# Three edits to a fused linear attention and bilinear feed-forward kernel: last block in pieces, paired early products, one block's stores on another queue

## The chip, the cores and the metric

The kernel runs on one core of a Trainium2 chip. The metric is device time in microseconds of one execution. The kernel before takes 296.92 us, the median of 6 runs (296.78 to 297.49).

## What is computed

Eight batches, eight heads, 576 positions, head size 64. Attention without a softmax, a normalisation per head, then a feed-forward part in which two projections are multiplied:

```python
kv  = einsum('bhsd,bhse->bhde', k, v)
o   = einsum('bhsd,bhde->bhse', q, kv)
o   = o / sqrt(mean(o*o, -1) + 1e-6) * g_norm
x   = o.transpose(0, 2, 1, 3).reshape(4608, 512)
out = ((x @ w_a) * (x @ w_b)) @ w_out        # 512 -> 1536 -> 512
```

Inputs and output are float32; the kernel multiplies in bfloat16 and float16 and sums in float32.

## The kernel before, in words

**Blocks.** The 4608 tokens are worked through in nine blocks of 512. Block 0 goes the plain way (`std_block`, line 387, and `o_std`, line 943). Blocks 1 to 8 use a fast 2x2 scheme with seven products instead of eight, called p1 to p7: `wino_block` (line 839) for x @ w_a and x @ w_b, and `o_unit` (line 1008) for the last product. The seven products need sums and differences of their operands, which VectorE makes beforehand: lines 746 (weights), 806 (tokens) and 993 (products of the two projections; four for each chunk, in the order s3, a21, s2, s4). ScalarE copies product banks out (`ev`, line 1040, and line 420), VectorE adds a bank to what was copied (`comb`, lines 1046 and 858).

**The output unit.** In `o_unit`, p6 is added in TensorE's bank on top of p1 after the bank has been copied out, p7 on top of p6, p3 on top of p5. The four output quarters are c11 = p1 + p2, c12 = p1 + p6 + p3, c21 = p1 + p6 + p7 + p4, c22 = p1 + p6 + p7 + p5. Each of the seven products has 12 matmuls of 128x256: two row halves ("subs") of six. The last block passes extra banks `W`, and takes the branch `if W:` (lines 1065 to 1093). There p7's sum is copied out by ScalarE (`e3`), p5's by ScalarE into `u5` (line 1076), and the quarters end with c22, c21 in two row halves, and c12 whole. `put` stores the quarters.

**Attention.** Batches 0 and 1 are loaded in a layout of 96 partitions (`early_batch`); TensorE transposes q (`early_qT_mm`, line 341, 12 transposes for a pair of heads) and multiplies k by v (`early_kv_mm`, line 325, 12 matmuls for a pair). Batches 2 to 7 are loaded by `load_node` over GpSimd's queue: q goes through a DRAM scratch tensor `scr` (line 661), k (lines 667, 668) and v (lines 673, 677) come straight. SyncE then turns the scratch into `qT` by a transposing DMA (line 682). The next batch's loads wait on GpSimd until `qT` of the batch before has landed (line 656). TensorE multiplies k by v (line 624), then q by the result (lines 353 and 539); ScalarE and VectorE normalise (lines 363, 371, 376).

**Order of the work.** The order on every engine is set by a small planner, `Plan`. Each piece is a node with an engine, a duration in us, a priority, what it depends on and the buffers that it takes and frees. `Plan.order` always picks the node that can start first on its engine, and among nodes that can start at once the one with the lowest priority number; the program is then written in that order, and each engine runs its part strictly in that order. `LAT` is the time that the planner adds between a node's end and its users. `EARLY_AT`, `W_AT`, `q_us` and `kv_us` are arrival times of data that the planner assumes. The semaphores of the real program are not touched by these numbers: they change the order alone.

**Banks.** The eight PSUM banks belong to three pools: banks 0 to 3 (rings `RX` and `RY`, two tiles each at most), bank 4 (`RO`), and banks 5 to 7 (`RQ` and `RS`, two each at most).

**Stores of block 0.** `o_std` stores four tiles of 128 rows on SyncE (line 964, through `store`, line 911). Because batch 0 has the 96-partition layout, each tile falls into two stores, eight in all.

Of the kernel before, what the change touches and what calls it, by code (L numbers as in the profile page):

```python
# [70 lines left out]


class Plan:
    LAT = {"PE": 0.27, "SP": 2.2, "ACT": 0.2, "DVE": 0.18}
    OWN = {"ACT": 0.12, "DVE": 0.13}

    def __init__(self, t0):
# [60 lines left out]
def kernel(  # L138
# [11 lines left out]
    nc = tc.nc  # L150
# [31 lines left out]
    NJ = FC // 2  # L182
# [226 lines left out]
    def act_us(n, bias=False):  # L409
        return (0.155 if bias else 0.06) + n / 1200  # L410
# [10 lines left out]
        ]  # L421

    T0 = 20.0
    B5, B6, CX, CY = 5, 8, 3, 4
    TB, TURN, AHEAD = 5, 3.0, 8.0
    plan = Plan({"PE": 5.7, "DVE": 3.3, "ACT": 2.7, "SP": 5.0, "POOL": 22.5, "V": 0.0})
# [62 lines left out]
    def early_batch(b, win):  # L489
        at = Attn(b)  # L490
        at.qt = [Buf(RKD).take()]
        at.kvd = at.qt[0].tile
        w0, w1 = win
        done = {}
        for p in range(NP):
            pr = w0 + (w1 - w0) * (p - 0.7) / NP
            sq, sk = (Buf(RX), Buf(RY)) if b == 0 else (Buf(RQ), Buf(RS))
            got = {n: plan.at(t) for n, t in zip("qkv", EARLY_AT[b][p])}
            if b == 0 and p == 0:
                for n in "qkv":  # L500
                    cast, eng, us = (
                        (nc.scalar.copy, "ACT", 0.75) if n == "k" else (nc.vector.tensor_copy, "DVE", 0.55)
                    )
                    got[n] = plan.add(
                        eng, us, pr - 1,
                        lambda n=n, cast=cast: cast(early[0][n][:, 0:2], raw[n]),
                        [got[n]],
                    )
            n1 = plan.add(
                "PE", 0.45, pr, lambda p=p, s=sq: at.early_qT_mm(p, s.tile), [got["q"]], [sq]  # L510
            )
            cp, eng, us = (nc.scalar.copy, "ACT", 0.56) if p % 2 and b else (nc.vector.tensor_copy, "DVE", 0.38)
            n2 = plan.add(
                eng, us, pr, lambda p=p, s=sq, cp=cp: at.early_qT_out(p, s.tile, cp),
                [n1], (), [sq],
            )
            n3 = plan.add(
                "PE", 0.40, pr, lambda p=p, s=sk: at.early_kv_mm(p, s.tile),
                [got["k"], got["v"]], [sk],
            )  # L520
            n4 = plan.add(
                "ACT", 0.45, pr,
                lambda p=p, s=sk: at.early_kv_out(p, s.tile, nc.scalar.copy), [n3], (), [sk],
            )
            done[p] = [n2, n4]
        slices(at, win, lambda p: done[p])
# [123 lines left out]
    def load_node(b, prio, dep, xt=None):  # L650
        ld = {"k": Buf(RK), "v": Buf(RV), "q": Buf(RQT)}
        scr = scr_pool.tile([NP, S, 2, D], BF16, name="scr", tag="scr")

        def issue():
            if dep is not None:
                nc.gpsimd.tensor_copy(gate_t, dep["q"].tile[0:1, 0, 0:1])
            if xt is not None:
                nc.gpsimd.tensor_copy(gate_t, xcols(NP - 1, (b - 2) * S, 1)[0:1])
            qv = q[b].rearrange("(p hl) s d -> hl s p d", hl=2)
            for hl in range(2):  # L660
                nc.gpsimd.dma_start(  # L661
                    out=scr[:, :, hl, :].rearrange("p s d -> s p d"), in_=qv[hl]
                )
            kt = ld["k"].tile
            ks = k[b, :, 0:SA, :].rearrange("h (sp c) d -> sp h c d", c=NCH)
            for c in range(NCH):
                nc.gpsimd.dma_start(out=kt[:, c], in_=ks[:, :, c, :])  # L667
            nc.gpsimd.dma_start(out=kt[0:SB, NCH], in_=k[b, :, SA:S, :].rearrange("h sp d -> sp h d"))
            for n, src in (("v", v),):
                t = ld[n].tile[:, 0 : H * (NCH + 1) * D].rearrange(  # L670
                    "p (h c d) -> p h c d", h=H, d=D
                )
                nc.gpsimd.dma_start(
                    out=t[:, :, 0:NCH, :],
                    in_=src[b, :, 0:SA, :].rearrange("h (sp c) d -> sp h c d", c=NCH),
                )
                nc.gpsimd.dma_start(
                    out=t[0:SB, :, NCH, :], in_=src[b, :, SA:S, :].rearrange("h sp d -> sp h d")
                )

        def transpose():
            nc.sync.dma_start_transpose(
                out=ld["q"].tile[:].rearrange("p a s -> p (a s)"),
                in_=scr[:].rearrange("a s h d -> (a s) (h d)"),
            )

        issue_us, q_us, ld["kv_us"] = (15.4, 4.3, 13.0) if dep is None else (9.0, 5.0 if b == 3 else 1.8, 16.0 if b == 3 else 13.0)

        ld["n"] = plan.add(
            "POOL", issue_us, prio, issue, ([(dep["qn"], 8.0)] if dep else []) + ([(xt, TURN)] if xt else []), [ld["k"], ld["v"]]  # L690
        )
        ld["qn"] = plan.add(
            "SP", 2.5, prio, transpose, [(ld["n"], q_us)], [ld["q"]]
        )
        return ld
# [234 lines left out]
    def o_std(ab, muls, win):  # L930
        w0, w1 = win
        ob = Buf(ROS)
        ng, copied = N0 // 128, []
        for g in range(ng):
            pr = w0 + (w1 - w0) * g / ng
            ps = Buf((RO, RY)[g % 2])

            n1 = None
            for f0 in range(0, FC, OP):

                def mm(g=g, ps=ps, f0=f0):
                    for fc in range(f0, f0 + OP):
                        nc.tensor.matmul(  # L943
                            ps.tile[:],
                            lhsT=ab.tile[:, fc, g * 128 : (g + 1) * 128],
                            rhs=wo_t[:, fc, :],
                            start=(fc == 0),
                            stop=(fc == FC - 1),
                        )

                n1 = plan.add(
                    "PE", mm_us(OP, d_model), pr + 0.01 * f0, mm,
                    [(wo_n, 5.8 if f0 + OP <= FC // 2 else 10.6), n1] + [muls[fc] for fc in range(f0, f0 + OP)],
                    [ps] if f0 == 0 else [], [ab],
                )
            o_reads.append(n1)
            n2 = plan.add(
                "ACT", act_us(d_model), pr,
                lambda g=g, ps=ps: nc.scalar.copy(ob.tile[:, g], ps.tile[:]),
                [n1] + copied[-1:], [ob] if g == 0 else [], [ps],  # L960
            )
            copied.append(n2)
            plan.add(
                "SP", 0.45, pr + 1, lambda g=g: store(g * 128, ob.tile[:, g]), [n2], (), [ob]
            )

    def o_unit(r0, ab, muls, osum, pr, du, chunks, pieces, m, w, first, second, X, Y, Z, ob, s2, s3, s4, W):
# [95 lines left out]
        t2, t3, t4 = (so_t[:, i] for i in range(3))  # L1063
        n1, n2, n3, n4 = osum
        if W:
            u5 = Buf(RU)
            p1 = prod(0, X, a11, b11, True, [], [X])
            e1 = ev(0, 0, 0, p1, [ob])
            p2 = prod(1, Y, a12, b21, True, [], [Y])
            c11 = comb(1, 0, 0, Y, [p2, e1], [Y])  # L1070
            p6 = prod(2, X, sx(s2), t2, False, [e1, n2], (), [s2], 2)
            e2 = ev(2, 0, 1, p6)
            p5 = prod(3, Z, a21, t1, True, [n1], [Z], (), 1)
            e5 = plan.add(
                "ACT", act_us(m * EH), pr + 3 * du,
                lambda: nc.scalar.copy(u5.tile[:, every], bank(Z, every)), [p5], [u5],
            )
            p7 = prod(4, X, sx(s3), t3, False, [e2, n3], (), [s3], 0)
            e3 = ev(4, 1, 0, p7)
            c22 = comb(4, 1, 1, X, [p7, e5], [X, u5], u=u5)  # L1080
            p3 = prod(5, Z, sx(s4), b22, False, [e5, n4], (), [s4], 3)
            c12 = comb(5, 0, 1, Z, [p3, e2], [Z])
            e1s, e2s = slice(0, EH), slice(EH, d_model)
            put(0, every, [c11], es=e1s)
            put(1, every, [c22], es=e2s)
            for i in range(m):
                put(0, slice(i, i + 1), [c12], queue=("SP", "ACT")[i], es=e2s)
            for i in range(m):
                subs = slice(i, i + 1)
                p4 = prod(6 + 0.1 * i, W[i], a22, t4, True, [n4], [W[i]], subs=subs)  # L1090
                c21 = comb(6 + 0.1 * i, 1, 0, W[i], [p4, e3], [W[i]], subs)
                put(1, subs, [c21], queue=("ACT", "SP")[i], es=e1s)
            return
        p1 = prod(0, X, a11, b11, True, [(wo_n, 10.6)], [X])
        e1 = ev(0, 0, 0, p1, [ob])
# [45 lines left out]
    for bi in range(1, nb + 1):  # L1141
# [10 lines left out]
        ab, muls = wino_block(bi, (st[bi], st[bi + 1]), wsum)  # L1152
    o_block(
        nb, ab, muls, osum, (st[nb + 1], st[nb + 1] + o_us[nb]), NJ // 2,
        (RO, RY, RY, RS, RQ), NJ // 2,
    )
    order, t = plan.order(), 5.7
    for n in order:
# [34 lines left out]
```

## Time and profile before

| | us |
|---|---|
| median of 6 runs | 296.92 |
| the profiled execution | 296.81 |
| its span, first to last instruction | 294.7 |
| outside the span | 2.1 |
| TensorE busy | 287.5 (98%) |
| VectorE busy | 240.1 (81%) |
| ScalarE busy | 191.5 (65%) |
| GpSimd busy | 77.3 (26%) |
| granted TensorE clock | 1.000 |

How to read it: PE is TensorE, PEld its weight loads, DVE VectorE, ACT ScalarE, POOL GpSimd, SP SyncE. In a timeline, a line starts with the start and the length in us of a run of like instructions; "SPq" is the issuing queue of SyncE. The duration of one matmul there includes its way through the array: those of 256 columns follow each other every 0.109 us although one is 0.273 us long. In the chain of waits, the chain that ended last, a line stands for the stretch that it adds to the path, so there the gap to the next line is counted and not the overlap.

### The profile page before, as it was taken

The page shows a single profiled execution, that of the slowest core. Times are in us where ns is not written, and L with a number is a line of the kernel's source. Part 1 is how long each engine was busy: PE and PEld are TensorE (multiplying, and loading weights), DVE is VectorE, ACT ScalarE, POOL GpSimd, SP SyncE. Part 2 cuts the span into 40 slices and gives each one's busy share as a digit, 9 for nine tenths or more (in the row PEclk, how much of TensorE's full clock was granted, in tenths as well). Part 3 has the DMA queues.
Part 4 walks back from the last instruction along what each step waited for, and adds up shares of the span by engine and source line. Part 5 has one row for each costly group of instructions (what it writes and reads, how often), then busy time and mean ns, then how long its engine had stood idle before and what let it go on. Part 6 is the DMA issues. An engine that isn't in the chain of part 4 may idle for free.

```text
span 294.7 us, 6757 instructions
## 1 busy us (share of the span) xinstructions
PE 287.5 (98%) x2646; PEld 237.8 (81%) x2648; DVE 240.1 (81%) x441; ACT 191.5 (65%) x395; POOL 77.3 (26%) x96
## 2 busy tenths in 40 slices
PE   7999999999999999999999999999999999999993
PEld 3645558965888988899988999898988888888882
DVE  5454879893987988789979999979989958788852
ACT  3757667866578677877757866786769546665420
POOL 8945830940191470380001910000000000000000
PEclk9999999999999999999999999999999999999999
DMA  8999999899999899599716999330165001200053
GB/s 178 199 199 200 196 158 167 114 169 186 207 102 168 139 179 170 43 140 209 170 32 148 143 167 168 81 145 20 40 84 166 2 0 44 101 2 0 9 172 107
DMA packets 112643, 36.26 MB, mean 123 GB/s; under 512 B 89060, under 2 KB 108516, under 8 KB 112612
## 3 DMA queue, kind: packets, MB, share of 16 engines
q0 software_dynamic: 77552, 18.44, 66.4%
q1 hardware_dynamic: 34448, 16.70, 26.6%
q10 hardware_dynamic: 612, 0.71, 0.8%
q8 instruction: 20, 0.33, 0.5%
q14 instruction: 11, 0.09, 0.1%
HBM read 37.75 MB, written 14.75 MB: 178 GB/s over the span
## 4 chain that ended last, share of the span: by engine, by line
PE 88%; DVE 4%; DMA 3%; POOL 2%; issue 1%; ACT 1%; DVEq 0%; ACTq 0%; POOLq 0%
PE bk L839 48%; PE bk L1008 24%; PE bk L387 7%; PE bk L943 3%; DMA wb_t<-in_moe_w_b_dram 3%; PE bk L624 2%; PE bk L353 1%; PE bk L367 1%; POOL as L242 1%; PE bk L539 1%; DVE c L858 1%; POOL so L242 1%; PE bk L341 1%; DVE so L746 1%; DVE o_sb L1046 1%
## 5 line engine op out<-in xcount | busy, mean ns | idle before, releaser
L858 DVE TENSOR_TENSOR c<-bk,u 128x512 f16<-128x512 f32 x144 | 96.4, 687 | 19.3 <-PE bk L839 11.8
L420 ACT COPY u<-bk 128x512 f32<-128x512 f32 x144 | 81.4, 591 | 36.5 <-PE bk L839 30.0
L839 PE MATMUL bk<-xp,wa_t 128*128 128x256 f16 x288 | 55.0, 273 | 0.1
L839 PE MATMUL bk<-xp,wb_t 128*128 128x256 f16 x288 | 55.0, 273 | 0.0
L839 PEld LDWEIGHTS <-wa_t 128*128 128x128 f16 x384 | 37.1, 98 | 5.7 <-issue 0.3
L1008 PEld LDWEIGHTS <-abt 128*128 128x128 f16 x384 | 37.5, 98 | 4.7 <-issue 0.3
L839 PEld LDWEIGHTS <-wb_t 128*128 128x128 f16 x384 | 37.6, 98 | 4.3
L1008 PE MATMUL bk<-wo_t,abt 128*128 128x256 f16 x288 | 37.2, 273 | 0.1
L839 PE MATMUL bk<-T,sb 128*128 128x256 f16 x192 | 36.6, 273 | 0.0
L839 PE MATMUL bk<-T,sa 128*128 128x256 f16 x192 | 36.6, 272 | 0.0
L420 ACT CAST c<-bk 128x512 f16<-128x512 f32 x48 | 28.0, 587 | 12.1 <-PE bk L839 11.5
L893 DVE TENSOR_TENSOR abt<-c 128x1024 f16<-128x1024 f16 x48 | 32.8, 687 | 0.9
L839 PEld LDWEIGHTS <-sb 128*128 128x128 f16 x288 | 28.2, 98 | 3.3
L839 PEld LDWEIGHTS <-sa 128*128 128x128 f16 x288 | 27.9, 98 | 3.5
L1008 PEld LDWEIGHTS <-as 128*128 128x128 f16 x288 | 28.1, 98 | 3.3
L1040 ACT COPY o_sb<-bk 128x512 f32<-128x512 f32 x31 | 18.2, 586 | 18.5 <-PE bk L1008 18.0
L376 DVE SCALAR_TENSOR_TENSOR xp<-bk,g_col,rs 128x288 f16<-128x288 f32 x40 | 20.3, 514 | 10.9 <-ACT rs L371 10.9
L1008 PE MATMUL bk<-so,as 128*128 128x256 f16 x192 | 25.2, 273 | 0.0
L371 ACT ACTIVATE rs<-bk,eps_t 128x288 f32<-128x288 f32 x40 | 20.0, 505 | 6.3 <-PE bk L367 6.1
L667 POOL DMA_DIRECT2D k_t<-in_k_dram x24 | 21.2, 900 | 0.8 <-issue 0.5
L661 POOL DMA_DIRECT2D scr<-in_q_dram x12 | 19.6, 1636 | 2.0 <-DMA wb_t<-in_moe_w_b_dram 0.9
L1046 DVE TENSOR_TENSOR o_sb<-bk,o_sb 128x512 f32<-128x512 f32 (+1 forms) x25 | 16.5, 666 | 3.0 <-PE bk L1008 2.3
(107 smaller groups left out, 428.5 us busy)
## 6 DMA issues: line engine op xcount, KB each, us to landing
out_dram<-o_sb SPq DMA_DIRECT2D x20, 256.0 KB, 2.7
scr<-in_q_dram POOLq DMA_DIRECT2D x12, 288.0 KB, 7.7
k_t<-in_k_dram POOLq DMA_DIRECT2D x24, 128.0 KB, 8.0
v_t<-in_v_dram POOLq DMA_DIRECT2D x6, 512.0 KB, 10.8
out_dram<-o_sb SPq DMA_DIRECT2D x18, 128.0 KB, 2.4
wa_t<-in_moe_w_a_dram POOLq DMA_DIRECT2D x6, 256.0 KB, 10.6
wb_t<-in_moe_w_b_dram POOLq DMA_DIRECT2D x6, 256.0 KB, 10.8
wo_t<-in_moe_w_out_dram POOLq DMA_DIRECT2D x2, 768.0 KB, 9.7
```

The source lines that it names most:

```text
L371: nc.scalar.activation(rs, self.s_ps[p, h][:, 0:HF], AF.Abs_reciprocal_sqrt, bias=eps_t)
L376: nc.vector.scalar_tensor_tensor(out=xcols(p, self.b * S + h * HF, HF), in0=self.x_ps[p, h][:, 0:HF], scalar=g_col, in1=self.rs[p, h], op0 ...
L387: nc.tensor.matmul(ps[:, 0:n], lhsT=w[:, kc, fc * 128 : (fc + 1) * 128], rhs=xcols(kc, 0, n), start=(kc == 0), stop=(kc == KC - 1),)
L420: ("ACT", act_us(n), lambda: nc.scalar.copy(*args())),
L661: nc.gpsimd.dma_start(out=scr[:, :, hl, :].rearrange("p s d -> s p d"), in_=qv[hl])
L667: nc.gpsimd.dma_start(out=kt[:, c], in_=ks[:, :, c, :])
L839: nc.tensor.matmul(ps.tile[:, i * n : (i + 1) * n], lhsT=lhs(w, sm)[:, kc, :], rhs=rhs()[:, kc, :], start=start and i == 0 and kc == 0, st ...
L858: lambda: nc.vector.tensor_add(cs(fi, h), full(ps), u.tile),
L893: nc.vector.tensor_mul(t, c[:, :, :, 0], c[:, :, :, 1])
L1008: nc.tensor.matmul(ps.tile[:, sub * EH : (sub + 1) * EH], lhsT=lhs(slice(j, j + 1))[:, 0, sub * 128 : (sub + 1) * 128], rhs=rhs[:, j, :], ...
L1040: lambda: nc.scalar.copy(o(fi, h), bank(X, every)), [dep], takes, frees,
L1046: nc.vector.tensor_add(o(fi, h, subs), bank(ps, subs), other)
```

## The change

**Tail in pieces.** In the last block's branch, p7 gets a bank `V` of its own and moves from place 4 to place 2.5 in the priorities; ScalarE's copy `e3` goes, and VectorE makes `c2x` = p7 + (p1 + p6) into the c21 quarter instead. p5 and p3 are done in two row halves in two banks `Z[0]`, `Z[1]`, p5's copy in two halves too. c22 becomes an addition of two SBUF operands, `c2x` and `u5`. p4 stands before p3, and c12 is made and stored in two halves, one on ScalarE's queue, one on SyncE's. The block takes seven banks instead of five.

**Two pairs at a time.** For batch 1, the transposes of two pairs of heads become one node (24 transposes), and the k-v products of two pairs too.

**Block 0's stores.** They go from SyncE to GpSimd's queue, with a planned 1.2 us each and a planned latency of 6.0. The planner's `kv_us` for batch 3 goes from 16.0 to 14.0.

```diff
-    LAT = {"PE": 0.27, "SP": 2.2, "ACT": 0.2, "DVE": 0.18}
+    LAT = {"PE": 0.27, "SP": 2.2, "ACT": 0.2, "DVE": 0.18, "POOL": 6.0}
...
+    P7_AT = 2.5
...
-            n1 = plan.add(
-                "PE", 0.45, pr, lambda p=p, s=sq: at.early_qT_mm(p, s.tile), [got["q"]], [sq]
-            )
+            if b == 0:
+                n1 = plan.add(
+                    "PE", 0.45, pr, lambda p=p, s=sq: at.early_qT_mm(p, s.tile), [got["q"]], [sq]
+                )
+            elif p % 2 == 0:
+                sq2 = Buf(RQ)
+                n1 = plan.add(
+                    "PE", 0.9, pr,
+                    lambda p=p, s=sq, s2=sq2: (at.early_qT_mm(p, s.tile), at.early_qT_mm(p + 1, s2.tile)),
+                    [got["q"]], [sq, sq2],
+                )
+            else:
+                sq = sq2
...
+            elif p % 2 == 0:
+                sk2 = Buf(RS)
+                n3 = plan.add(
+                    "PE", 0.8, pr,
+                    lambda p=p, s=sk, s2=sk2: (at.early_kv_mm(p, s.tile), at.early_kv_mm(p + 1, s2.tile)),
+                    [got["k"], got["v"]], [sk, sk2],
+                )
+            else:
+                sk = sk2
...
-        issue_us, q_us, ld["kv_us"] = (15.4, 4.3, 13.0) if dep is None else (9.0, 5.0 if b == 3 else 1.8, 16.0 if b == 3 else 13.0)
+        issue_us, q_us, ld["kv_us"] = (15.4, 4.3, 13.0) if dep is None else (9.0, 5.0 if b == 3 else 1.8, 14.0 if b == 3 else 13.0)
...
-                "SP", 0.45, pr + 1, lambda g=g: store(g * 128, ob.tile[:, g]), [n2], (), [ob]
+                "POOL", 1.2, pr + 1, lambda g=g: store(g * 128, ob.tile[:, g], nc.gpsimd), [n2], (), [ob]
...
-            u5 = Buf(RU)
+            u5, V, Z = Buf(RU), W[0], [Z, W[1]]
+            W = W[2:]
+            rows = [slice(i, i + 1) for i in range(m)]
...
-            e2 = ev(2, 0, 1, p6)
-            p5 = prod(3, Z, a21, t1, True, [n1], [Z], (), 1)
-            e5 = plan.add(
-                "ACT", act_us(m * EH), pr + 3 * du,
-                lambda: nc.scalar.copy(u5.tile[:, every], bank(Z, every)), [p5], [u5],
-            )
-            p7 = prod(4, X, sx(s3), t3, False, [e2, n3], (), [s3], 0)
-            e3 = ev(4, 1, 0, p7)
-            c22 = comb(4, 1, 1, X, [p7, e5], [X, u5], u=u5)
-            p3 = prod(5, Z, sx(s4), b22, False, [e5, n4], (), [s4], 3)
-            c12 = comb(5, 0, 1, Z, [p3, e2], [Z])
+            e2 = ev(2, 0, 1, p6, (), [X])
+            p7 = prod(P7_AT, V, sx(s3), t3, True, [n3], [V], [s3], 0)
+            c2x = plan.add(
+                "DVE", dve_us(m * EH), pr + 4 * du,
+                lambda: nc.vector.tensor_add(o(1, 0), bank(V, every), o(0, 1)), [p7, e2], (), [V],
+            )
+            e5 = []
+            for i in range(m):
+                p5 = prod(3 + 0.1 * i, Z[i], a21, t1, True, [n1], [Z[i]], (), 1, subs=rows[i])
+                e5.append(
+                    plan.add(
+                        "ACT", act_us(EH), pr + 3 * du,
+                        lambda i=i: nc.scalar.copy(u5.tile[:, rows[i]], bank(Z[i], rows[i])),
+                        [p5], [] if i else [u5],
+                    )
+                )
+            c22 = plan.add(
+                "DVE", dve_us(m * EH), pr + 4.2 * du,
+                lambda: nc.vector.tensor_add(o(1, 1), o(1, 0), u5.tile[:, every]), [c2x] + e5, (), [u5],
+            )
...
             for i in range(m):
-                put(0, slice(i, i + 1), [c12], queue=("SP", "ACT")[i], es=e2s)
+                p4 = prod(5 + 0.1 * i, W[i], a22, t4, True, [n4], [W[i]], subs=rows[i])
+                c21 = comb(5 + 0.1 * i, 1, 0, W[i], [p4, c22], [W[i]], rows[i])
+                put(1, rows[i], [c21], queue=("ACT", "SP")[i], es=e1s)
             for i in range(m):
-                subs = slice(i, i + 1)
-                p4 = prod(6 + 0.1 * i, W[i], a22, t4, True, [n4], [W[i]], subs=subs)
-                c21 = comb(6 + 0.1 * i, 1, 0, W[i], [p4, e3], [W[i]], subs)
-                put(1, subs, [c21], queue=("ACT", "SP")[i], es=e1s)
+                p3 = prod(6 + 0.1 * i, Z[i], sx(s4), b22, False, [e5[i], n4], (), [s4], 3, subs=rows[i])
+                c12 = comb(6 + 0.1 * i, 0, 1, Z[i], [p3, e2], [Z[i]], rows[i])
+                put(0, rows[i], [c12], queue=("ACT", "SP")[i], es=e2s)
...
-        (RO, RY, RY, RS, RQ), NJ // 2,
+        (RO, RY, RS, RY, RS, RQ, RY), NJ // 2,
```

More of the change, by code (lines that the diff above doesn't have):

```diff
@@ L516, in early_batch @@
             )
-            n3 = plan.add(
-                "PE", 0.40, pr, lambda p=p, s=sk: at.early_kv_mm(p, s.tile),
-                [got["k"], got["v"]], [sk],
-            )
+            if b == 0:
+                n3 = plan.add(
+                    "PE", 0.40, pr, lambda p=p, s=sk: at.early_kv_mm(p, s.tile),
+                    [got["k"], got["v"]], [sk],
+                )
+            elif p % 2 == 0:
+                sk2 = Buf(RS)
+                n3 = plan.add(
+                    "PE", 0.8, pr,
[4 more added lines that the diff above has]
+                sk = sk2
             n4 = plan.add(
```

## The prediction

> **What bounds the kernel now.** I read the page's busy times first, then the chain of waits by time, then the timeline at the three places that the diff touches.
>
> ```profile
> PE 287.5 (98%) x2646; PEld 237.8 (81%) x2648; DVE 240.1 (81%) x441; ACT 191.5 (65%) x395; POOL 77.3 (26%) x96
> PE 88%; DVE 4%; DMA 3%; POOL 2%; issue 1%; ACT 1%; DVEq 0%; ACTq 0%; POOLq 0%
> ```
>
> TensorE (PE) is busy nearly always, and 88% of the chain lies on it. From 16.2 us, when the first weights are there, to 289.66, when its last matmul ends, it hardly pauses. The exceptions that I find are the places where it goes from small products back to block 0's, one gap at 80.66 to 80.93 behind a VectorE (DVE) chain, and a like one at 225.7. So a change can win in three ways only: less time on TensorE, fewer such gaps, or a shorter end after 289.66. The span ends at 294.7, thus 5.0 us come behind the last matmul.
>
> The chain of waits at the end:
>
> ```profile
> 280.28 8.09 PE bk L1008 x74
> ...
> 288.39 0.59 ACT o_sb L1040
> ...
> 289.01 1.02 DVE o_sb L1046 x2
> 290.03 0.33 DVEq L1188
> 290.36 0.60 DVE o_sb L1046
> ```
>
> The reader is to see that TensorE is packed (74 matmuls in 8.09 us, 0.109 each) up to 288.37, and that the end then does not hang on its last 12 matmuls (p3, to 289.66) but on ScalarE's copy of p7 and VectorE's queue behind it. The timeline, with narrow windows for the last additions:
>
> ```profile
> 288.19 1.47 PE L1008 MATMUL bk<-wo_t,as 128*128 128x256 f16 x12
> 289.01 0.69 DVE L1046 TENSOR_TENSOR o_sb<-bk,u 128x512 f32<-128x512 f32 x1 [3.80 <-ACT o_sb L1040]
> 289.62 0.41 DVE L1046 TENSOR_TENSOR o_sb<-bk,o_sb 128x256 f32<-128x256 f32 x1
> 290.28 0.68 DVE L1046 TENSOR_TENSOR o_sb<-bk,o_sb 128x512 f32<-128x512 f32 x1
> 290.11 1.29 ACTq L911 DMA_DIRECT2D out_dram<-o_sb  x2
> ```
>
> c22 at 289.01, c21 in halves at 289.62 and 289.95, c12 at 290.28 to 290.96: c12's product was there at 289.66, and it waits 0.62 us for VectorE and then takes 0.68. Slots, start to start, are 0.60 for 512 columns and 0.33 for 256.
>
> **Part 1, the tail.** TensorE's count stays: seven products of 12 matmuls. Removed is ScalarE's copy of p7 (0.58); p5's copy (0.58) becomes two, each priced between 0.36 (the nearest short ScalarE copy, L639) and 0.58. Added on VectorE is c2x (0.69, one slot of 0.60); c12 becomes two halves of 0.41. The SBUF-only c22 has no row; between 0.42 (a 512-column float16 sum) and 0.69 (a float32 one with a PSUM operand) I take 0.69, the row of its own type.
>
> p7 in a bank of its own needs no copy of p6 before it, and s3 is the first sum that VectorE makes (282.29 to 282.71), so p7 can be done well before the end. With p4 and p3 last, 24 matmuls or 2.62 us follow p5. VectorE's queue behind p5 is: second half copy 0.36, c22 0.60, two halves of c21 0.66, first half of c12 0.33, in all 1.95. It is 0.67 us ahead of TensorE, so the last half of c12 starts when p3 ends: 289.66 + 0.02, plus 0.41, gives 290.09 instead of 290.96, a gain of 0.87.
>
> Six or fewer matmuls of p4 done earlier, as filling work, cost nothing; each further one brings p5 0.109 closer to the end, and all twelve leave a gain of 0.87 - 0.65 = 0.22. Before, p4 did fill (8 of its 12 before 282.5), because p2 had to wait for a bank of 0 to 3. Now p5's halves have banks 5 to 7, so 8 matmuls of p5 are there to fill instead; I take no loss.
>
> Behind the additions: stores of 128 KB landed after 1.7 to 2.2 us. Six of them were issued between 289.73 and 291.5; now four are out before the last half. That is worth 0 to 0.3; I take 0.05. ScalarE's queue holds only the two stores behind c21 and c12, SyncE's last one waits for nothing else. **Sum: -0.9, between -0.2 and -1.2.**
>
> **Part 2, pairs.** The chain of waits around batch 1's transposes:
>
> ```profile
> 20.55 0.49 PE bk L341 x12
> 21.04 0.97 PE bk L387 x4
> 22.00 0.49 PE bk L341 x12
> 22.49 1.40 PE bk L387 x6
> ...
> 40.95 2.16 PE bk L387 x10
> ```
>
> Ten matmuls of L387 take 2.16, so one takes 0.216. Behind each run of transposes the next run is longer than that: 0.97 - 0.86 and 1.40 - 1.30, 0.10 each time; at 31.45 and 32.69 the same. The transposes themselves cost 0.49 either way. Two runs in one spare one return, twice: -0.2. The k-v products were already 24 in a row (23.89 and 33.66), so there the change finds nothing. The second pair's transposes need a second bank of 5 to 7 at 30.9: if it is the one that VectorE frees at 31.77 and not the one that ScalarE frees at 31.22, TensorE, which gets there at 31.45, waits 0.3. Nothing else hides it: TensorE has its weights over a microsecond ahead (issued 23.17, landing after 10.8, used at 35.30). **Sum: -0.2, between -0.2 and +0.1.**
>
> **Part 3, the stores.** SyncE's and GpSimd's (POOL's) timelines:
>
> ```profile
> 67.45 0.79 SPq L911 DMA_DIRECT2D out_dram<-o_sb  x2
> 68.36 6.03 SPq L682 DMA_TRANSPOSE qT<-scr  x1
> 74.48 4.32 SPq L911 DMA_DIRECT2D out_dram<-o_sb  x6
> ```
>
> ```profile
> 66.47 0.69 POOL L677 DMA_DIRECT2D v_t<-in_v_dram  x1 [1.31 <-DMA scr<-in_q_dram]
> 79.94 0.38 POOL L656 COPY gate_t<-qT 1x1 bf16<-1x1 bf16 x1 [12.79 <-DMA qT<-scr]
> ```
>
> GpSimd has nothing to do from 67.16 to 79.94. Eight issues there cost 0.69 to 0.82 each (rows of L677 and L704), 5.5 to 6.6 in all. They wait for ScalarE's four copies, of which the last ends at 75.51; two issues behind it end at 77.1. Queued behind them is only the gate of batch 4's loads, which waits for batch 3's qT until 79.94 anyway: cover 2.8 us. The tile that they read is wanted again only for block 2. On SyncE the transposing DMA can start when the scratch has landed (issued 55.37, 12.4 to landing: 67.8), 0.6 earlier at most; nobody on the path waits for it.
>
> The page "DMA: Bandwidth & Descriptors" of the Trainium skill, section "SWDGE vs HWDGE vs iDMA", speaks against this edit: a plain transfer belongs on SyncE's or ScalarE's queue, since GpSimd writes its descriptors in software and VectorE can lock it out meanwhile; "SBUF — State Buffer" tells of 620 ns that became 3100. By that the eight issues would be an estimated 25 us, end past 92 and push batch 4's loads by over 12 us. The trace does not agree: from 55 to 60 us GpSimd's issues ran beside a VectorE that was 90% busy, at 0.88 each as elsewhere.
>
> The planned 14.0 moves batch 3's k-v products up by 2.0, from 79.11 to about 77.1. The last piece of V was issued at 66.47 and landed after 10.7, at 77.2; other V loads took 8.9 to 11.7, so 75.4 to 78.2. The stores no longer share the DMA engines ahead of it. TensorE waits 0 to 1.1; I take 0. Against that, the gap of 0.27 at 80.66 may close, as batch 3's products are then there to fill it. **Sum: 0, between -0.3 and +1.1.**
>
> **Total.** -0.9 - 0.2 + 0 = -1.1. Against the profiled execution, 296.81 (294.7 of span and 2.1 around it), that is 295.7; the median lies 0.11 higher, at 296.92, and gives 295.8.
>
> **Rivals.** About 0.2%, or 0.6 us, is what can be told from no change: 296.33 to 297.51.
>
> *V is late.* TensorE stands before batch 3's k-v products until 78.2 instead of 77.1: -1.1 + 1.1, the time stays at 296.9. For it speaks the margin of -0.1; against it the lighter DMA load. Chance 0.07.
>
> *The tail's queue stays on VectorE.* All of p4 fills early, p5 and c22 come late, the tail gains 0.22: 296.92 - 0.2 - 0.2 = 296.5. For it: p4 did fill before. Against it: four products stand ahead of it now. Chance 0.07. This is also the case in which the change does not do what it says.
>
> *Slower: batch 3's normalising crowds VectorE.* From 72.4 to 82.0 VectorE works without a pause and the chain of waits runs through it (72.36 to 80.89) until TensorE gets its input at 80.93. If batch 3's attention comes earlier, its eight normalising operations (L376, slot 0.43, now from 85.12 on) can come in front of the sums that TensorE waits for. Each costs 0.43 there; from four on, +1.7 eats the gain and leaves 296.92 - 1.1 + 1.7 = 297.5; all eight would give 299.2. Against it: qT lands at 79.3 at the earliest, and two microseconds earlier brings them to 83. Chance 0.14, with any other disorder that a newly planned order brings in at this point.
>
> *More:* the gap at 80.66 closes (-0.27) and the last stores land 0.25 sooner: 295.3. Chance 0.10.
>
> **Numbers.** The forecast has 0.62. Faster by over 0.2%: 0.62 + 0.10 = 0.72. Within: 0.07 + 0.07 = 0.14. Slower: 0.14. The range is 295.0 to 297.6: below, the best case with 0.3 to spare; above, the start of the slower case, most of whose 0.14 I leave out.
>
> **What would show it.** After: no ScalarE copy behind p7; the last VectorE addition has 256 columns and starts within 0.1 us of the last matmul's end; last matmul to span's end 4.1 instead of 5.0. Around 21 and 31 us, 24 transposes in one run of 0.98. Eight issues of L911 on GpSimd between 67 and 77.5, the gate at 79 to 80. Wrong would be a TensorE pause at 77, a last matmul later than 289.7, or a changed tail order with p4 ahead of p5.

## The result, and the profile after

The changed kernel takes 298.47 us (median of 17 runs, 297.59 to 300.71), the kernel before 297.17 in the same sessions (36 runs). The ratio is 1.0049, 95% interval 1.0037 to 1.0061: slower by 0.5%, where 1.1 us faster was forecast. The profiled execution took 297.98, its span is 296.2 against 294.7.

The page of the changed kernel, busy times and the chain's shares:

```profile
PE 287.2 (97%) x2646; PEld 237.7 (80%) x2648; DVE 241.2 (81%) x443; ACT 192.9 (65%) x395; POOL 82.3 (28%) x104
PE 68%; DMA 22%; POOL 4%; ACT 1%; DVE 1%; issue 1%; DVEq 0%; ACTq 0%; SPq 0%; POOLq 0%
```

TensorE has the same 2646 matmuls and the same busy time; what is new is that 22% of the chain that ended last is now DMA, where it was 3%. The last part of it in the chain of waits (start, length, what):

```profile
54.02 1.58 POOL scr L682
55.60 12.20 DMA scr<-in_q_dram
...
67.86 14.04 DMA qT<-scr
...
81.95 0.41 PE bk L353 x2
```

Batch 3's transposing DMA is issued at 67.86, lands 14.0 later, and TensorE's first q product of batch 3 starts when it has landed. Before, the same DMA took 11.5 and TensorE did not wait for it. (Lines have moved: 353 is as before, 600 is now 621, 656 is 677, 839 is 860, 911 is 932, 1008 is 1029, 1040 is 1061, 1046 is 1067; in this chain 682 is the load of q, formerly 661, and the transposing DMA is 703.) TensorE's timeline at that place:

```profile
80.14 0.38 PE L860 MATMUL bk<-T,wb_t 128*128 128x256 f16 x2
81.95 0.41 PE L353 MATMUL bk<-qT,kvd 128*128 128x288 bf16 x2 [1.43 <-DMA qT<-scr]
```

Two matmuls from 80.14 have their slots (0.109 each) until 80.36. TensorE then stands for 1.6 us, although "PE busy" for 80 to 85 us, 3.57 of 5, shows less of it, because the last matmul counts as busy for its whole 0.273 us and not for its slot alone. Such pauses are best taken from starts: the next start, less the last start, less one slot. All of them above 0.06 us, behind the first weights, give this account of the two profiled executions:

| us | before | after | difference |
|---|---|---|---|
| first transposes of batch 1 start | 20.48 | 20.75 | +0.27 |
| pauses at batch 1's transposes and products | 12 of 0.09 to 0.10 | 8 | -0.38 |
| pause at 80 | 0.27 | 1.60 | +1.33 |
| pauses at 193 | 0.07 | 0.93 | +0.86 |
| pause at 227 | 0.27 | 0.22 | -0.05 |
| last matmul starts | 289.39 | 291.37 | +1.98 |
| from there to the span's end | 5.27 | 4.83 | -0.44 |
| outside the span | 2.15 | 1.78 | -0.37 |

The first row is scatter of the first loads (20.5 to 21.1 in the runs below). The rest sums to +1.76 for TensorE, -0.44 for the tail and -0.37 outside the span. The last is no scatter: outside the span every run of the change takes 1.7 to 2.0 us, and so do those of e3, e7, e9 and e10 below, while every run of the kernel before and of the other experiments takes 2.1 to 2.4. No run shows why.

The two pauses at 193, of 0.51 and 0.42, are no waits for batch 3's data. TensorE's timeline of the changed kernel shows what ended each:

```profile
193.80 0.38 PE L860 MATMUL bk<-xp,wa_t 128*128 128x256 f16 x2 [0.34 <-DVE o_sb L1067]
...
194.65 0.38 PE L860 MATMUL bk<-T,wa_t 128*128 128x256 f16 x2 [0.25 <-ACT u L420]
```

The first waits for an addition of VectorE that empties a bank; the addition itself could start only when its product was done:

```profile
193.06 0.69 DVE L1067 TENSOR_TENSOR o_sb<-bk,o_sb 128x512 f32<-128x512 f32 x1 [1.38 <-PE bk L1029]
```

The second waits for ScalarE:

```profile
190.87 0.59 ACT L1061 COPY o_sb<-bk 128x512 f32<-128x512 f32 x1 [0.45 <-PE bk L1029]
191.35 2.78 ACT L621 ACTIVATE xp<-xp,g_col 128x576 f16<-128x576 f16 x4
194.03 1.06 ACT L420 COPY u<-bk 128x512 f32<-128x512 f32 x2
```

ScalarE first waits for an output bank, then does four scalings of a later batch in one piece (2.78 us), and only then the copy that TensorE needs. In the kernel before the output copy stood behind the scalings (190.08, then 193.22). So the same instructions stand in a different order; that this makes the two pauses is read from the waits, and no run moves these instructions alone.

The early transposes and the tail do what the change says. TensorE's timeline around 21 us:

```profile
20.75 0.81 PE L341 MATMUL bk<-ident,abt 96*64 96x96 bf16 x24
21.49 1.04 PE L387 MATMUL bk<-xp,wb_t 128*128 128x512 f16 x4
```

and VectorE's at the end, where c22 (line 1113) is followed by the four halves:

```profile
289.96 0.69 DVE L1113 TENSOR_TENSOR o_sb<-o_sb,u 128x512 f32<-128x512 f32 x1 [0.15 <-ACT u L1107]
290.75 1.42 DVE L1067 TENSOR_TENSOR o_sb<-bk,o_sb 128x256 f32<-128x256 f32 x4
```

The last addition ends at 292.17, 0.80 behind the start of the last matmul; before it was 1.57. (Since p3 is added in the bank that already holds p5, the quarter c12 is p1 + p6 + p5 + p3, before and after, not p1 + p6 + p3.)

### The profile page after: what moved, and what is told of

Read it like the earlier page. It is cut to its first block, busy times and chain, and to the rows that moved or that the text cites. A ratio compares the mean times of both kernels' runs of the same rounds, so it can differ in the third digit from the quotient of the medians.

```text
span 296.2 us, 6781 instructions
## 1 busy us (share of the span) xinstructions
PE 287.2 (97%) x2646; PEld 237.7 (80%) x2648; DVE 241.2 (81%) x443; ACT 192.9 (65%) x395; POOL 82.3 (28%) x104
## 4 chain that ended last, share of the span: by engine, by line
PE 68%; DMA 22%; POOL 4%; ACT 1%; DVE 1%; issue 1%; DVEq 0%; ACTq 0%; SPq 0%; POOLq 0%
PE bk L860 41%; PE bk L1029 23%; DMA scr<-in_q_dram 8%; DMA qT<-scr 8%; DMA wb_t<-in_moe_w_b_dram 4%; DMA wa_t<-in_moe_w_a_dram 3%; PE bk L645 2%; POOL as L242 1%; PE bk L560 1%; POOL scr L682 1%; ACT xp L621 1%; PE bk L353 1%; POOL so L242 1%; PE bk L367 1%; POOL wo_t L725 1%
## 5 line engine op out<-in xcount | busy, mean ns | idle before, releaser
L420 ACT COPY u<-bk 128x512 f32<-128x512 f32 x144 | 81.2, 591 | 35.5 <-PE bk L860 31.5
L1061 ACT COPY o_sb<-bk 128x512 f32<-128x512 f32 x30 | 17.6, 588 | 13.1 <-PE bk L1029 12.4
```

The source lines that it names most:

```text
L420: ("ACT", act_us(n), lambda: nc.scalar.copy(*args())),
L1061: lambda: nc.scalar.copy(o(fi, h), bank(X, every)), [dep], takes, frees,
```

## The experiments

Each of the parts, and the two halves of the third part, can be had alone. The plan is computed from the numbers in the source, so a planned time changes only the order, and a store's issuing engine can be changed without touching the order. The traces show what each edit reorders on TensorE: the tail the last block alone; the pairs the products around batch 1's alone; the stores' queue nothing (e4 against before, e2 against e1, the change against e3); the planned 14.0 the order from batch 3's products on, to the last block.

### e1 to e4: two planned times by two queues

All but e4 hold the tail and the pairs. e1 leaves the third part out, e2 is the change with 16.0, e3 the change with SyncE as the issuing engine:

```diff
e2:
-        ... (9.0, 5.0 if b == 3 else 1.8, 14.0 if b == 3 else 13.0)
+        ... (9.0, 5.0 if b == 3 else 1.8, 16.0 if b == 3 else 13.0)
e3, and the other way round in e4, which is otherwise the kernel before:
-                "POOL", 1.2, pr + 1, lambda g=g: store(g * 128, ob.tile[:, g], nc.gpsimd), [n2], (), [ob]
+                "POOL", 1.2, pr + 1, lambda g=g: store(g * 128, ob.tile[:, g]), [n2], (), [ob]
```

> The tail and the pairs of the change; block 0's stores on SyncE and the planned 16.0 as before. Two theories. QUEUE: block 0's stores on GpSimd's queue run beside batch 3's transposing DMA and hold it up (qT landed at 81.9 instead of 79.8), and TensorE waits for it. ORDER: the planned 14.0 brings batch 3's q products 1.3 us forward in TensorE's own order and reorders what follows, and the pauses at 80.5 and 193 come from that order. Both expect neither pause here: 297.17 - 0.38 (pairs, four transitions of 0.09 to 0.10) - 0.45 (the tail as measured) = 296.3, ratio 0.997. If the pauses come from the tail or the pairs, 298.

> The change with the planned 16.0 instead of 14.0: the stores stay on GpSimd's queue, the order of the middle is that of before. QUEUE: qT still lands at 81.9; TensorE reaches the first q product of batch 3 at 82.24 - 0.38 = 81.9, so a pause of 0 to 0.3 at 82 and none at 193: 296.3 to 296.6. ORDER: qT lands at 79.8 to 80, no pause: 296.3. The landing of qT tells them apart, not the time.

> The order of the change on TensorE, ScalarE and VectorE to the instruction, but block 0's stores are issued by SyncE. QUEUE: qT lands at 79.8 again, the pause at 80.5 goes (-1.4) and that at 193 (0.9) stays: 298.47 - 1.4 = 297.1, ratio 1.000. ORDER: both pauses stay: 298.4, ratio 1.004.

> The kernel before with one thing changed: block 0's stores are issued by GpSimd, the order on every other engine is that of before. QUEUE: qT lands at about 81.9 instead of 79.8; TensorE reaches its user at 82.24, so the time stays within 0.2% of 297.17, 297.0 to 297.5, and the next batches' loads start 2 us later. ORDER: qT lands at 79.3 to 79.8 and the time stays too.

| with tail and pairs | stores on SyncE | stores on GpSimd |
|---|---|---|
| planned 16.0: median, ratio to before | e1: 294.96, 0.9919 (0.9893 to 0.9945) | e2: 295.28, 0.9936 (0.9913 to 0.9958) |
| gate of batch 4 opens, that is qT has landed | 79.6 | 81.4 |
| pause at 80, pauses at 193 | 0.27, 0.07 | 0.26, 0.07 |
| planned 14.0: median, ratio to before | e3: 296.77, 0.9985 (0.9969 to 1.0001) | the change: 298.47, 1.0049 (1.0037 to 1.0061) |
| gate opens | 80.2 | 82.0 |
| pause at 80, pauses at 193 | 0.20 at the k-v products, 0.92 | 1.60, 0.93 |

e4 takes 297.23, ratio 1.0003 (0.9986 to 1.0020). Its gate, on GpSimd's timeline:

```profile
81.81 0.18 POOL L656 COPY gate_t<-qT 1x1 bf16<-1x1 bf16 x1 [2.28 <-DMA qT<-scr]
```

and TensorE's timeline of e3 where the change has its pause of 1.60 (the same order, the stores on SyncE):

```profile
80.69 0.38 PE L860 MATMUL bk<-T,wb_t 128*128 128x256 f16 x2
80.91 0.41 PE L353 MATMUL bk<-qT,kvd 128*128 128x288 bf16 x2
```

So QUEUE is right about the landing: GpSimd's queue delays qT by 1.8 to 1.9 us in every pair. It is right about the pause at 80 too, which e3 loses at the same TensorE order. But it takes both: with 16.0 TensorE comes so late that the later landing costs nothing that can be told (e1 and e2 overlap; e4 equals before). ORDER is right about the other part: 14.0 alone costs 1.8 us (e3 against e1: 2.2 more of span, 0.4 less outside it), the pauses at 193 (0.85) and the tail (0.83) among it. The whole third part costs 3.5 us (the change against e1); 1.7 of it is the queue at 14.0 (the change against e3). And e1 is faster than forecast for the whole change.

### e5 and e6: tail alone, pairs alone

> The tail edit alone; the order of everything before the last block is that of before. If the two parts simply add, this is e1 without the pairs: -1.5 us, 295.5, ratio 0.995, last matmul's start to span's end 3.8 instead of 5.3. If the tail's gain needs the pairs, less.

> The pairs alone; all other order is that of before. TensorE's pauses between block 0's products and the transposes go from eight to four of 0.09 to 0.10: -0.38 us, 296.7, ratio 0.9987; the gap at 80.5 and the end stay as they are. If a wait for data takes the saving, ratio 1.000.

e5 takes 295.59, ratio 0.9948 (0.9935 to 0.9961); from the last matmul's start to the end 3.82. e6 takes 296.55, ratio 0.9978 (0.9969 to 0.9988); its pauses at the transposes and products are eight of 0.09 to 0.10, all others as before. Both as expected; -0.52% and -0.22% make -0.74%, and e1 has -0.81%, which the intervals allow. But e6's time falls by 0.65 us where the pauses account for 0.38, and e7 below falls as far with TensorE's order untouched. So the worth of the pairs stands on the pauses, 0.38; the time alone does not show it.

### e7: block 0's stores left out

```diff
-                "SP", 0.45, pr + 1, lambda g=g: store(g * 128, ob.tile[:, g]), [n2], (), [ob]
+                "SP", 0.45, pr + 1, lambda g=g: None, [n2], (), [ob]
```

> The kernel before without the eight stores of block 0: rows 0 to 511 of the output are not written. It asks what those stores cost batch 3's transposing DMA when they are issued by SyncE. QUEUE: on SyncE six of the eight stand behind the transposing DMA in the same queue and hardly touch it, so without them qT lands at 79.0 to 79.8, little earlier than 79.8, while on GpSimd's queue it landed at 81.3 to 81.9. If bytes alone counted, leaving 1 MB out (about 5 us at 200 GB/s of which it shares part) would bring qT to 77.5 or earlier. Time within 0.2% of 297.0 either way, since no wait of TensorE hangs on it.

The gate opens as if the stores were there:

```profile
79.81 0.61 POOL L656 COPY gate_t<-qT 1x1 bf16<-1x1 bf16 x1 [12.10 <-DMA qT<-scr]
```

On SyncE the stores cost the transposing DMA nothing: 11.5 us to landing with them, 11.3 without. The rates tell why. From 76 to 78 us, the stretch's last two columns are the DMA engines' busy share and GB/s; the kernel before, then the change:

```profile
76.00:78.00 2.00, 2.00 (x20) 1.78 (x19) 2.00 (x4) 1.76 (x4) 0.00 (x0) 1.00 2.00 198
```

```profile
76.00:78.00 2.00, 2.00 (x24) 1.80 (x22) 2.00 (x4) 1.65 (x4) 0.67 (x2) 1.00 1.48 281
```

With GpSimd's queue 281 GB/s move (342 in e4), 164 without the stores: the stores' bytes go through while the transposing DMA is under way. On SyncE six of the eight stand behind it: issued from 74.5 on, they landed from 80.1 on, behind qT at 79.8. The time of e7 was a miss: 296.53, ratio 0.9977 (0.9966 to 0.9988), where within 0.2% was expected. Of the 0.7 us, 0.4 lies outside the span (1.8 against 2.1, as in the change) and the rest in the span (294.8 in the median, 295.1 before), though TensorE's pauses are those of before; the cause stays open.

### e8: the last block's stores of c21 and c22 left out

```diff
-            put(1, every, [c22], es=e2s)
...
-                put(1, subs, [c21], queue=("ACT", "SP")[i], es=e1s)
```

> The kernel before without the last block's stores of c21 and c22 (their sums are made, the lower half of its rows is not written), so only c11's and c12's stores are left. It asks why the tail gained 1.5 and not 0.9: from the last addition to the span's end before took 3.70, e1 3.04. If stores issued in a bunch land later, this takes 3.0 to 3.2 and the time is 296.4 to 296.6, ratio 0.998; if the landing depends on the size or shape of the last additions and not on the bunch, it stays 3.7 and 297.1.

From the last addition to the end 3.15 instead of 3.70, with the same additions; 296.67, ratio 0.9982 (0.9971 to 0.9993). The bunch it is: before, six stores of 128 KB moved at 254 to 348 GB/s from 290.5 to 293.0, and with two stores instead of six the end came 0.55 sooner. In e1 they are spread, and the tail's additions and stores run like this (all engines' timeline):

```profile
287.08 0.69 DVE L1113 TENSOR_TENSOR o_sb<-o_sb,u 128x512 f32<-128x512 f32 x1
287.73 1.47 PE L1029 MATMUL bk<-wo_t,as 128*128 128x256 f16 x12
287.88 1.13 DVE L1067 TENSOR_TENSOR o_sb<-bk,o_sb 128x256 f32<-128x256 f32 x3
289.24 0.42 DVE L1067 TENSOR_TENSOR o_sb<-bk,o_sb 128x256 f32<-128x256 f32 x1 [0.23 <-PE bk L1029]
```

The last half of c12 waits for TensorE and not the other way round, ends at 289.67, and the span ends 3.08 later. Under 14.0 four of p4's twelve matmuls are done early, c22 comes 0.4 closer to the end, the six stores bunch again, and the last addition is followed by 3.84 (e3) and 4.03 (the change).

### e9: the pause moved by one number

```diff
-        ... (9.0, 5.0 if b == 3 else 1.8, 14.0 if b == 3 else 13.0)
+        ... (9.0, 7.0 if b == 3 else 1.8, 14.0 if b == 3 else 13.0)
```

> The change with one more number, the planned q_us of batch 3 at 7.0 instead of 5.0: on TensorE one group of four matmuls (0.44) and two more go ahead of batch 3's first q products, which start 0.66 of work later; everything else stands as in the change. The place of TensorE times the landing of qT should decide: place 80.4 + 0.66 = 81.0 against a landing at 81.9, so the pause goes from 1.6 to 0.9 and the time from 298.47 to about 297.8, ratio 1.002. ORDER alone (a pause that does not depend on the landing): no change, 1.0045. The pause at 193 and the tail stay.

297.45, ratio 1.0023 (1.0010 to 1.0036): the expected size, but not at the expected place. TensorE's timeline:

```profile
79.46 0.38 PE L645 MATMUL bk<-v_t,k_t 128*128 128x128 bf16 x4 [0.74 <-DMA v_t<-in_v_dram]
```

In this execution the last piece of V landed at 79.4 (issued 67.10, 12.3 to landing), later than the 77.3 of the change, and TensorE stood 0.91 us before the last four k-v products. It then came to the q products when qT had landed. So the expected size is luck: 0.91 for V where 0.9 for qT was foreseen. Place against landing decided here too, but under 14.0 there are two landings to miss. That of V's last piece varies: over all profiles it came between 77.0 and 79.6, whichever queue had the stores, and in e3 it made the 0.20. How often the change's own runs miss it is not shown, since one of them was profiled.

### e10 and e11: planned 18.0 and 15.0

```diff
e10, on e1:
-        ... 16.0 if b == 3 else 13.0)
+        ... 18.0 if b == 3 else 13.0)
e11, on e1:
+        ... 15.0 if b == 3 else 13.0)
```

> Tail and pairs, stores on SyncE, but the planned arrival of batch 3's K and V is 18.0: batch 3's products come 2.2 of work later instead of 1.3 earlier. From batch 3 on the order of the rest differs from e1 in over 1600 lines and resembles that of the change (568 lines apart); ScalarE has the output copy ahead of the scalings near 193, as the change has. If the loss of 1.8 us under 14.0 came from being early, this is as fast as e1, 295.0. If it came from which order the planner falls into afterwards, the pause at 193 (0.8) is here too and the time is 295.8 to 296.8, although batch 3 is later than ever.

> Tail and pairs, stores on SyncE, planned arrival 15.0: batch 3's products come 0.65 of work earlier than in e1, and the order falls back to that of e1 afterwards (196 lines apart instead of 1556). If the order that follows decides, it is as fast as e1, 294.8 to 295.2; if each microsecond of earliness costs, half of the 1.8, 295.9.

e11 takes 295.07, ratio 0.9928 (0.9916 to 0.9940): as fast as e1, although batch 3 comes earlier. e10 takes 296.96, ratio 0.9993 (0.9980 to 1.0005), a little beyond what was expected: pauses of 0.75 at 79, 0.39 at 107, 0.40 at 178, 0.51 at 193, and 4.26 from the last matmul's start to the end. Later is as dear as earlier. Of e10's loss against e1, 0.5 lies at 79, where batch 3 was moved; the other 1.8, in pauses and in the tail, lies behind it. So it is mostly not the 2 us that cost, but the order into which the planner falls from there to the end.

### e12: block 0's stores on ScalarE

```diff
-                "SP", 0.45, pr + 1, lambda g=g: store(g * 128, ob.tile[:, g]), [n2], (), [ob]
+                "SP", 0.45, pr + 1, lambda g=g: store(g * 128, ob.tile[:, g], nc.scalar), [n2], (), [ob]
```

> The kernel before with block 0's eight stores issued by ScalarE, whose queue is not GpSimd's software one, and not the queue of the transposing DMA either. If any other queue runs beside the transposing DMA and delays it, qT lands at 81.3 to 82 as with GpSimd; if it is GpSimd's queue alone, at 79.8. ScalarE spends about 8 times 0.4 = 3.2 us on the issues, so the time may rise by up to 2 us for that reason; only the landing is asked for.

qT lands 15.1 after its issue, at 83.4: another hardware queue delays it as GpSimd's does, so it is not the software queue as such. The time, 306.73, ratio 1.0319 (1.0301 to 1.0337), is a miss with a plain cause, on ScalarE's timeline:

```profile
84.31 1.07 ACT L420 COPY u<-bk 128x512 f32<-128x512 f32 x2 [8.02 <-DMA qT<-scr]
```

The program gives each DMA one of eight semaphores in turn and lets it wait for the one that had it before. The seventh store had that of the transposing DMA, so ScalarE stood 8 us before it could issue that store, and TensorE 7.7. That is not yet the 9.6 that e12 loses. While TensorE stood, its granted clock fell to 0.50, from 81.2 to 88.1, as the stretch from 86 to 87 us shows (the clock is the third number from the end):

```profile
86.00:87.00 1.00, 1.00 (x6) 0.70 (x5) 0.39 (x1) 0.73 (x2) 1.00 (x1) 0.50 0.76 56
```

Until then matmuls of 256 columns follow each other every 0.213 us instead of 0.109, which costs another 1.5.

## Why the prediction was wrong, point by point

**What bounds the kernel: right.** TensorE's packed stream was the whole matter; the account above closes to 0.1 us. (The second gap stands at 226.4, not at 225.7.)

**Part 1, the tail: right in kind, too small.** With the order that I had in mind (e1) the last addition came 0.74 behind the last matmul's start instead of 1.57: 0.83 against the forecast 0.87. The term "I take 0.05" for the landing of the last stores was mis-sized: e1 measures 0.62 (3.08 instead of 3.70), and e8 shows that the bunch makes it. The tail is worth 1.45, beyond the bound of 1.2. In the change it gave only 0.44, since 14.0 filled in four matmuls of p4, which by the working was to cost nothing, and the stores bunched again: the last addition came 0.80 behind the last matmul's start instead of 1.57, but the end behind it took 4.03 instead of 3.70.

**Part 2, the pairs: right in kind, half the size.** I priced the return from the transposes, 0.10 each, and missed that going to them pauses as well, 0.09. Four pauses go, -0.38 instead of -0.2.

**Part 3, the stores: here it failed.** It was put at 0, at most +1.1, and cost 3.5. Three steps failed. "On SyncE the transposing DMA can start when the scratch has landed, 0.6 earlier at most" looked at the start only; it started 0.5 earlier and landed 2.1 later. "Nobody on the path waits for it" was read from the trace of before, where TensorE came to it at 82.24; but the same edit brings the q products forward, which I had worked out for the k-v products only. Place 80.4 and landing 81.9 cross. And "Against that, the gap of 0.27 may close" took the 14.0 as a move of one product, while it replans all that follows: 0.9 at 193 and 1.0 of the tail's gain.

**The rule that I weighed.** "DMA: Bandwidth & Descriptors" (the Trainium skill, "SWDGE vs HWDGE vs iDMA") spoke against GpSimd's queue, and I set it aside since its issues were not slow. They were not: eight issues of 0.50 to 0.56, done by 78.1. The edit cost time nevertheless, by what the transfers met and not by what issuing them took. The same page's section "Issuing engines are not separate DMA queues" says that DMAs run on the same 16 DMA engines and interleave, whoever issues them, and that issuing from several engines saves issue time only. The interleaving agrees with the 281 GB/s above. That only issue time is at stake does not: the queue also decided what stood in front of what, with 2 us at the landing.

**The rivals.** *V is late* named a wait of TensorE at this place for data of this batch; it was qT in the change's profile, V in e9 (0.91) and e3 (0.20). *The tail's queue stays on VectorE* came true by a third: four of p4's matmuls filled early, not twelve, and the tail gave 0.44; but what took the rest was the landing of the stores, not VectorE's queue. *Slower: batch 3's normalising crowds VectorE* got the sign, but at 80 TensorE waited for qT and not for VectorE. Its last clause, any other disorder of a newly planned order, comes nearer, only that the disorder stood at 193 and in the tail and not at this point.

## What to carry to other kernels

Where one engine is packed, price an edit of the order by two columns for each thing that it moves: when the engine now arrives, and when the data now lands, with every transfer that the edit puts beside it. A number in a planner is not a wait but an order: look how many instructions it moves before believing that it moves one. And take the parts of a change alone: here tail and pairs together run at 294.96, 0.8% below before, and the third part hid it.

## What the runs showed of the hardware

A transposing DMA of 11.3 to 12.0 us to landing took 13.1 to 14.0 with 1 MB of stores on GpSimd's queue beside it and 15.1 with them on ScalarE's, but was untouched when six of the eight stood behind it in its own queue (11.3 without any). There is one profile of each kernel. With six stores of 128 KB issued within 2 us at the end of the program, the span ended 3.70 us behind the last addition; with the same six spread 3.08, with two of them 3.15. In e12, where TensorE stood for 7.7 us, its granted clock was 0.50 from 4 us after its last matmul had started until 3 us after it went on. TensorE pauses 0.09 to 0.10 both before and after a run of 96x96 transposes or 96x64 products amid products of 128 rows.
